# Cutting 33 unread matrix products into 99 narrower ones ahead of the first expert

## The chip, the cores and the metric

The kernel runs on one core of a Trainium2 chip. The metric is the device time of one execution in microseconds (us). Three runs of the kernel before gave 690.85, 692.42 and 748.87 us; their median is 692.42 us. The profiled execution took 690.02 us by the same measure, and 688.4 us of it is the span from the first to the last instruction, so 1.6 us lie around the span.

## The reference, cut to what matters

Two parts follow each other. The first is attention over 8 batches, 8 heads, 576 positions and 64 dimensions, once over positions averaged in fours and once over a narrow band; the second is a mixture of experts on its 4608 rows of 512 numbers:

```python
x = np.ascontiguousarray(attn_out.transpose(0, 2, 1, 3)).reshape(B * S, H * D)
...
logits = x @ w_gate
order = np.argsort(-flat)
for idx in order:                       # greedy, at most cap = N // E = 576 rows for each expert
    ...
    assigned[tok] = e
...
for e in range(E):
    mask = assigned == e
    h = np.maximum(x[mask] @ w1[e], 0.0)
    out[mask] = h @ w2[e]
```

Which row goes to which expert depends on all logits together: an expert that is full passes its rows on. All 8 experts end with 576 rows each.

## The kernel before, in words

The first 244 us of the trace are attention; it leaves the rows x in the chip's main memory and their logits in on-chip memory. Then come eight units, one for each expert that becomes full, in the order in which they do. A unit has four stages. Its **routing** (`Routing.phase`) finds the threshold of the next full expert by counting: comparisons on VectorE (L879), counts as small products on TensorE into the tile pR (L933, L951, L979), and a rank and a list of rows (L990, L991, L1202). Its **gathering** (`Experts.gather`) fetches 576 rows of x by the list in five indirect transfers (`xg`, L1326, issued by GpSimd), turns them with products against the identity (L1343, into pX) and splits them into two 16-bit parts (`xt`, high on ScalarE L1347, low on VectorE L1348). Its **weights** arrive by their own transfers and are split likewise (`wh` L1306, `wl` L1309). Its **products** (`mlp`) are the first layer (L1390, into pH, with the split of its result on ScalarE L1421 and VectorE L1424) and the second (L1438, into pX), whose results are scattered to the output (L1448).

For the first unit nothing can be hidden behind an earlier one: routing is a chain that alternates between VectorE and TensorE, then rows have to be fetched, then turned. In that stretch the kernel gives TensorE products that nobody reads. `Routing.busy` (L905) puts 5 and 8 of them between the last steps of the routing, each 128 x 128 against 288 columns. `Experts.spin` (L1286) puts 33 more of the same size behind the list of rows: 28 ahead of the turning of the first 128 rows, and 5 behind it, ahead of the first real product. They multiply a tile of ones (`one`) with the table `codes` and write one half of a pH buffer, from which nothing is read. This is what "first gathering" and "unread products" mean in this document.

A scheduler sets the order of the instructions on each engine from priorities and dependences. Dependences that only fix the order on one engine are added by hand; those around the change are:

```python
for a, b in ((ex.spins[0], ex.turns[0]), (ex.turns[0], ex.spins[1])):
    for mm in b:
        ro.behind_(mm, a[-1])
...
ro.behind_(ex.products[0], ex.spins[1][-1])
```

So TensorE does the 28, then the four turning products of the first rows (`turns[0]`), then the 5, then the first real product (`products[0]`). pH has two buffers: the first belongs to the 13 unread products of the routing and then to the first real products (f = 0); the second belongs to the 33 unread products and then to the products for f = 1, which therefore wait until the last of the 33 has ended.

Of the kernel before, what the change touches and what calls it, by code (L numbers as in the profile page):

```python
# [1222 lines left out]
class Experts:  # L1223
# [62 lines left out]

    def spin(self, a, b):
        p = self.ps.tile([128, 2, 512], F32, name="pH", bufs=2)
        n = b.shape[1] * b.shape[2]
        mm = [self.nc.tensor.matmul(p[:, 0, :n], a, b.rearrange("p e t -> p (e t)"), start=True, stop=True)  # L1290
              for _ in range(sum(SPIN))]
        self.spins = mm[:SPIN[0]], mm[SPIN[0]:]

    def split(self, raw, first):
# [175 lines left out]
LEAD = -19.0  # L1470
PACE = (0.6, 4, 10.5, 13, 15.3, 17, 18.5, 19.2, 21.5, 24, 26.5, 30, 32.5, 36.5, 37.2, 43.9, 43)
PACES = {2: (8.5, 12.8, 15.8, 17.4, 19.1, 20.7, 22.1, 23, 24.7, 26.5, 28.5, 31, 33, 36.5, 37.2, 43.9, 43)}
SPIN = (28, 5)


def moe_attention(tc, q, k, v, wg, w1, w2, cst, out):
# [173 lines left out]
```

## Time and profile before

| what | us |
|---|---|
| profiled execution | 690.02 |
| its span | 688.4 |
| runs | 690.85, 692.42, 748.87 |
| TensorE busy in the span | 646.2 (94%) |
| VectorE busy | 510.6 (74%) |
| ScalarE busy | 331.9 (48%) |
| attention, up to the first routing | 0 to 244 |
| first routing | 244 to 266 |
| first gathering and turning | 266 to 278 |
| units back to back on TensorE | 278 to 681 |

How to read the rows: times are microseconds from the start of the span, durations of single instructions are nanoseconds. PE is TensorE's product, PEld its load of the 128 x 128 stationary tile, which runs beside products; DVE is VectorE, ACT ScalarE, POOL GpSimd. The ends of products are modelled: a product's duration includes its way through the array, and the next one starts before it ends, so the rate of a row of products is read from their starts. PEclk is the clock granted to TensorE as a share of 2.4 GHz; it takes two levels, 0.50 (1.2 GHz) and 1.00. A timeline row such as "x8" merges eight instructions that follow each other.

### The profile page before, as it was taken

What the parts mean: (1) busy time and instruction counts of PE and PEld (TensorE: products, weight loads), DVE (VectorE), ACT (ScalarE), POOL (GpSimd) and SP (SyncE); (2) the same over time, 40 slices, a digit from 0 to 9 for tenths busy, and PEclk for the clock granted to TensorE, in tenths of its full rate; (3) what the DMA queues carried; (4) which work ended last, traced back from release to release, by engine and by line L of the source; (5) the groups of instructions that cost most, each with busy time, mean ns of one, the idle gap of its engine ahead of it and who ended that gap; (6) DMA issues with size and microseconds to landing.
All of it is one profiled execution on the core that took longest, in us unless ns stands there. A gap on an engine that the chain in (4) does not pass through costs nothing.

```text
span 688.4 us, 21563 instructions
## 1 busy us (share of the span) xinstructions
PE 646.2 (94%) x8781; PEld 454.4 (66%) x8781; DVE 510.6 (74%) x1475; ACT 331.9 (48%) x648; POOL 246.2 (36%) x332
## 2 busy tenths in 40 slices
PE   7999999999899948999999999999999999999993
PEld 5778788788777835765764764764764765755841
DVE  5588889878889887997888896896896966534500
ACT  4578777788676413525325434424424424433410
POOL 4698586676827504005005104113013025011011
PEclk9799999999999957999999999999999999999997
DMA  9988978879857714406339159067067089634001
GB/s 271 223 198 231 242 199 231 233 198 241 239 159 194 230 40 142 173 15 229 141 119 287 47 222 207 24 247 183 25 260 169 25 283 249 233 39 99 2 30 38
DMA packets 138505, 113.87 MB, mean 165 GB/s; under 512 B 89126, under 2 KB 116006, under 8 KB 138408
## 3 DMA queue, kind: packets, MB, share of 16 engines
q1 hardware_dynamic: 130648, 89.71, 47.4%
q0 software_dynamic: 6752, 22.03, 10.3%
q8 instruction: 69, 1.13, 0.7%
q10 hardware_dynamic: 1008, 0.77, 0.4%
q14 instruction: 28, 0.23, 0.1%
HBM read 85.94 MB, written 19.46 MB: 153 GB/s over the span
## 4 chain that ended last, share of the span: by engine, by line
PE 56%; issue 17%; DVE 14%; ACT 6%; POOL 3%; DMA 2%; SPq 0%; POOLq 0%; ACTq 0%; DVEq 0%
PE pX L1438 17%; PE pH L1390 14%; PE g L596 4%; PE s L550 3%; PE g L344 2%; PE pR L933 2%; PE g L575 2%; POOL out_dram L1448 2%; PE g L616 2%; ACT kt L328 2%; DVE wl L1309 1%; POOL xg L1326 1%; DVE qt L326 1%; PE g L420 1%; DVE cmp L879 1%
## 5 line engine op out<-in xcount | busy, mean ns | idle before, releaser
L1390 PE MATMUL pH<-xt,wh 128*128 128x320 f16 (+2 forms) x1040 | 192.0, 284 | 1.1 <-PE pH L1290 0.7
L1438 PE MATMUL pX<-wh,ht 128*128 128x512 f16 (+1 forms) x640 | 178.7, 380 | 0.0
L1438 PEld LDWEIGHTS <-ht 128*128 128x128 f16 (+1 forms) x960 | 83.0, 100 | 93.5 <-issue 2.6
L1390 PE MATMUL pH<-xt,wl 128*128 128x320 f16 (+2 forms) x520 | 144.3, 284 | 0.1
L1438 PE MATMUL pX<-wl,ht 128*128 128x512 f16 (+1 forms) x320 | 117.8, 380 | 0.0
L1390 PEld LDWEIGHTS <-wh 128*128 128x128 f16 x1040 | 98.1, 98 | 29.2 <-issue 4.9
L1448 POOL DMA_INDIRECT out_dram<-y,idx x40 | 40.5, 1012 | 177.0 <-ACT y L1445 119.0
L1421 ACT ACTIVATE ht<-pH 128x512 f16<-128x512 f32 (+1 forms) x128 | 45.5, 407 | 114.7 <-PE pH L1390 114.7
L1309 DVE SCALAR_TENSOR_TENSOR wl<-nat,wh 128x512 f16<-128x512 f32 x128 | 83.5, 685 | 15.5 <-ACT wh L1306 13.3
L1445 ACT ACTIVATE y<-pX 128x512 f32<-128x512 f32 (+1 forms) x40 | 23.8, 594 | 104.1 <-issue 54.1
L1424 DVE SCALAR_TENSOR_TENSOR ht<-pH,ht 128x512 f16<-128x512 f32 (+1 forms) x128 | 52.3, 449 | 26.2 <-ACT ht L1421 25.7
L1306 ACT ACTIVATE wh<-nat 128x1024 f16<-128x1024 f32 (+1 forms) x68 | 67.6, 1002 | 4.3 <-DMA nat<-in_moe_w_dram 4.3
L1326 POOL DMA_INDIRECT xg<-x_dram,idx x40 | 42.5, 1062 | 62.8 <-DVE idx L1219 48.6
L1390 PEld LDWEIGHTS <-wl 128*128 128x128 f16 x520 | 50.2, 98 | 12.6 <-DVE wl L1309 0.4
L585 ACT COPY pt<-g 64x512 f32<-64x512 f32 x71 | 41.2, 580 | 25.2 <-PE g L575 20.4
L596 PE MATMUL g<-vw,pt 128*64 128x65 f32 x1152 | 43.1, 225 | 2.7 <-ACT kt L328 0.8
L596 PEld LDWEIGHTS g<-vw,pt 128*64 128x64 f32 x1152 | 37.6, 137 | 8.6 <-issue 3.0
L1093 POOL MEMSET f<- 128x1 bf16 x8 | 0.8, 106 | 111.9 <-DVE sumf L987 41.1
L344 PE MATMUL g<-ident,nat 128*128 128x128 f32 x256 | 38.9, 281 | 0.2 <-DMA nat<-in_k_dram 0.2
L1355 DVE SCALAR_TENSOR_TENSOR xs<-xg,xs 128x512 f16<-128x512 f32 (+1 forms) x30 | 20.1, 688 | 25.4 <-ACT xs L1354 23.2
L328 ACT COPY kt<-g 64x512 f32<-64x512 f32 (+1 forms) x58 | 35.5, 613 | 6.6 <-PE g L344 5.8
L550 PE MATMUL s<-kt,qt 64*32 64x38 f32 x2304 | 30.2, 206 | 6.2 <-issue 4.8
(242 smaller groups left out, 1132.9 us busy)
## 6 DMA issues: line engine op xcount, KB each, us to landing
nat<-in_moe_w_dram SPq DMA_DIRECT2D x28, 1024.0 KB
vw<-in_v_dram SPq DMA_DIRECT2D x136, 78.0 KB
x_dram<-x SPq DMA_DIRECT2D x36, 256.0 KB
nat<-in_q_dram SPq DMA_DIRECT2D x32, 256.0 KB
nat<-in_k_dram SPq DMA_DIRECT2D x32, 256.0 KB
nat<-in_v_dram SPq DMA_DIRECT2D x28, 256.0 KB
up<-up_dram SPq DMA_DIRECT2D x9, 256.0 KB
nat<-in_moe_w_dram POOLq DMA_DIRECT2D x2, 1024.0 KB
```

Source lines behind the costliest of these rows:

```text
L328: self.nc.scalar.copy(out, in_)
L344: nc.tensor.transpose(p[:, a, :, fp], src[:, 4 * hh + 2 * a + s, 2 * fp:2 * fp + 2].rearrange("p f d -> p (f d)"), self.ident)
L550: nc.tensor.matmul(sv[32 * hp:32 * hp + 32, i, c], qt[r, hp, QW * w:QW * w + QW], kt[r, hp, key0(w):key0(w) + KW], start=False, stop=True, ...
L596: nc.tensor.matmul(o[64 * i:64 * i + 64, 65 * h:65 * h + 65], pt[:, 2 * (h % 2) + i, 2 * g + h // 2].rearrange("p b q -> p (b q)"), self.v ...
L1306: self.wh.append(nc.scalar.activation(hi[:, a:b], r[:, a:b], AF.Copy, scale=sc))
L1309: self.wl = nc.vector.scalar_tensor_tensor(lo[:, a:a + LOP], r[:, a:a + LOP], sc, hi[:, a:a + LOP], op0=OP.mult, op1=OP.subtract)
L1326: self.fetched = nc.gpsimd.indirect_dma_start(out=xg[:n], out_offset=None, in_=self.x, in_offset=bass.IndirectOffsetOnAxis(ap=idx[:n, c:c ...
L1390: mm = nc.tensor.matmul(p[:, s, o:o + s1 - s0], w[d][a][:, 128 * f:128 * f + 128], xt[:, b, d, s0:s1], start=j == 0, stop=j == len(seq) - 1)
L1421: last = nc.scalar.activation(hi, q, AF.Relu)
L1424: low = nc.vector.scalar_tensor_tensor(lo, q, 0.0, hi, op0=OP.max, op1=OP.subtract)
L1438: mm = nc.tensor.matmul(p[o:o + m], ht[:, f, h0:h0 + m], w[4 + f // 2][b][:, 512 * (f % 2):512 * (f % 2) + 512], start=j < parts, stop=j > ...
L1448: i = nc.gpsimd.indirect_dma_start(out=self.out, in_=y[:n], in_offset=None, out_offset=bass.IndirectOffsetOnAxis(ap=idx[:n, c:c + 1], axis=0))
```

## The change

The 288 columns of `codes` are taken in three thirds of 96 columns. Each of the 33 products becomes three, each with its own load of the same stationary tile: 84 ahead of the first turning and 15 behind it. They write the three thirds of the same 288 columns of pH. The number of columns that stream through the array is the same (33 x 288 = 99 x 96 = 9504).

```diff
     def spin(self, a, b):
         p = self.ps.tile([128, 2, 512], F32, name="pH", bufs=2)
-        n = b.shape[1] * b.shape[2]
-        mm = [self.nc.tensor.matmul(p[:, 0, :n], a, b.rearrange("p e t -> p (e t)"), start=True, stop=True)
-              for _ in range(sum(SPIN))]
+        n = b.shape[1] * b.shape[2] // CUTS
+        flat = b.rearrange("p e t -> p (e t)")
+        mm = [self.nc.tensor.matmul(p[:, 0, n * (k % CUTS):n * (k % CUTS) + n], a, flat[:, n * (k % CUTS):n * (k % CUTS) + n],
+                                    start=True, stop=True) for k in range(sum(SPIN))]
         self.spins = mm[:SPIN[0]], mm[SPIN[0]:]
...
-SPIN = (28, 5)
+CUTS = 3
+SPIN = (28 * CUTS, 5 * CUTS)
```

Line numbers of the changed kernel are higher by one behind L1290. On TensorE, around the turning of the first rows, the order before is this (`one` is the tile of ones, `xg` the fetched rows):

```order
L1290 LDWEIGHTS one
L1290 MATMUL pH<-codes,one 128x288
L1343 MATMUL pX<-ident,xg 128x128 x4
L1290 LDWEIGHTS one
L1290 MATMUL pH<-codes,one 128x288
```

and after the change:

```order
L1291 LDWEIGHTS one
L1291 MATMUL pH<-codes,one 128x96
L1344 MATMUL pX<-ident,xg 128x128 x4
L1291 LDWEIGHTS one
L1291 MATMUL pH<-codes,one 128x96
```

The turning stays where it was between the two groups; what stands on either side are 84 and 15 pairs of a load and a product in place of 28 and 5.

The scheduler also moves a few neighbours. On ScalarE, behind the first piece of `xt`, the order before is (`xh` and `xl` are tables of the second routing, copied in two halves each):

```order
L1347 ACTIVATE xt<-pX 128x4x128
L1047 COPY xh<-s 128x288
L1347 ACTIVATE xt<-pX 128x4x128
L1047 COPY xh<-s 128x288
L1047 COPY xl<-s 128x288 x2
L1347 ACTIVATE xt<-pX 128x4x128 x2
```

and after the change:

```order
L1348 ACTIVATE xt<-pX 128x4x128
L1047 COPY xh<-s 128x288 x2
L1047 COPY xl<-s 128x288
L1348 ACTIVATE xt<-pX 128x4x128
L1047 COPY xl<-s 128x288
L1348 ACTIVATE xt<-pX 128x4x128 x2
```

Two of the copies pass from behind the second piece of `xt` to ahead of it. On VectorE, at the end of the first f of the first unit, the order before is (`less` and `flag` are steps of the second routing, `ht` the low part of the layer's result):

```order
L1059 TENSOR_TENSOR oh<-eq,amu 128x288
L943 TENSOR_TENSOR less<-cap,pR 64x8
L1424 SCALAR_TENSOR_TENSOR ht<-pH,ht 128x512
L1424 SCALAR_TENSOR_TENSOR ht<-pH,ht 128x64
L946 TENSOR_TENSOR flag_5647<-pR,less 64x8
```

and after the change:

```order
L1059 TENSOR_TENSOR oh<-eq,amu 128x288
L1425 SCALAR_TENSOR_TENSOR ht<-pH,ht 128x512
L1425 SCALAR_TENSOR_TENSOR ht<-pH,ht 128x64
L943 TENSOR_TENSOR less<-cap,pR 64x8
L946 TENSOR_TENSOR flag_5647<-pR,less 64x8
```

The two `ht` steps pass ahead of `less`. On TensorE the small products of the second routing keep their order and stand behind one to three more products of the first layer, up to the fourth f; from there on, and on GpSimd and SyncE throughout, the orders are the same.

## Rows read from the trace of the kernel before

**Rows 1.** The page: busy time, then 40 slices of the span, tenths.

```profile
PE 646.2 (94%) x8781; PEld 454.4 (66%) x8781; DVE 510.6 (74%) x1475; ACT 331.9 (48%) x648; POOL 246.2 (36%) x332
PE   7999999999899948999999999999999999999993
PEclk9799999999999957999999999999999999999997
```

**Rows 2.** Chain of waits, 266 to 284 us: start, us, what.

```profile
266.54 3.95 DMA xg<-x_dram,idx
...
270.54 0.66 PE pX L1343 x4
271.19 1.74 PE pH L1290 x5
...
272.98 0.38 PE pH L1390 x4
273.36 0.46 PE pX L1343 x4
273.84 0.61 ACT xt L1347
274.47 0.69 DVE xt L1348
...
277.13 0.48 PE pX L1343 x4
277.63 0.39 ACT xt L1347
...
278.06 2.20 PE pH L1390 x15
```

**Rows 3.** The 33 products alone: count, durations in ns, first and last start.

```profile
L1290 PEld LDWEIGHTS <-one x33: 97/98/147, 264.8 to 271.4; 128*128 128x128 bf16 x33
L1290 PE MATMUL pH<-codes,one x33: 286/286/444, 264.8 to 271.5; 128*128 128x288 bf16 x33
```

**Rows 4.** Timeline, 261 to 274 us: start, us, engine, line, idle before and releaser.

```profile
261.98 2.11 PE L905 MATMUL pH<-codes,one 128*128 128x288 bf16 x8
...
264.80 5.08 PE L1290 MATMUL pH<-codes,one 128*128 128x288 bf16 x28
...
270.54 0.66 PE L1343 MATMUL pX<-ident,xg 128*128 128x128 f32 x4 [0.66 <-DMA xg<-x_dram,idx]
...
271.03 0.78 PE L1290 MATMUL pH<-codes,one 128*128 128x288 bf16 x5
...
271.23 0.60 ACT L1347 ACTIVATE xt<-pX 128x512 f16<-128x512 f32 x1 [2.95 <-issue]
...
271.88 0.38 PE L1390 MATMUL pH<-xt,wh 128*128 128x128 f16 x4
...
272.98 0.38 PE L1390 MATMUL pH<-xt,wh 128*128 128x128 f16 x4 [0.72 <-PE pH L1290]
```

**Rows 5.** Stretches: PE, PEld, DVE, ACT, POOL busy, PEclk, DMA share, GB/s.

```profile
260.00:262.00 2.00, 1.53 (x9) 0.65 (x8) 1.64 (x9) 0.00 (x0) 0.00 (x0) 0.50 0.00 0
...
266.00:267.00 1.00, 1.00 (x6) 0.63 (x5) 0.25 (x1) 0.98 (x3) 0.46 (x1) 0.50 0.51 195
267.00:268.00 1.00, 1.00 (x6) 0.61 (x5) 1.00 (x3) 1.00 (x3) 0.69 (x2) 0.57 0.00 0
268.00:269.00 1.00, 1.00 (x11) 0.80 (x9) 1.00 (x3) 0.28 (x1) 0.88 (x1) 1.00 0.72 156
...
273.50:276.00 2.50, 2.50 (x41) 2.48 (x40) 1.53 (x5) 2.07 (x5) 2.24 (x4) 1.00 0.73 205
```

**Rows 6.** The 33 products in a slow and a fast stretch: first and last start.

```profile
L1290 PE MATMUL pH<-codes,one x6: 444/444/444, 265.5 to 266.7; 128*128 128x288 bf16 x6
...
L1290 PE MATMUL pH<-codes,one x10: 286/286/286, 268.5 to 269.6; 128*128 128x288 bf16 x10
```

**Rows 7.** Timeline of TensorE: narrower products, each with its own load.

```profile
21.44 2.66 PE L772 MATMUL g<-wm 128*64 128x64 bf16 x46
...
253.54 0.65 PE L933 MATMUL pR<-ol,level 128*128 128x16 bf16 x18 [1.09 <-DVE ol L1125]
...
273.64 0.61 PE L1390 MATMUL pH<-xt,wl 128*128 128x128 f16 x8
...
274.09 0.61 PE L1390 MATMUL pH<-xt,wh 128*128 128x128 f16 x8
```

**Rows 8.** Stretches of the attention, PE alone: PE busy, PEclk, DMA share, GB/s.

```profile
18.70:22.10 3.40, 2.28 (x79) 0.50 1.16 205
22.10:25.50 3.40, 3.40 (x45) 0.50 0.99 263
25.50:29.00 3.50, 3.50 (x57) 1.00 1.05 189
```

**Rows 9.** Timeline, ScalarE, VectorE and TensorE at the moved steps.

```profile
273.84 0.60 ACT L1347 ACTIVATE xt<-pX 128x512 f16<-128x512 f32 x1 [1.64 <-PE pX L1343]
274.34 0.42 ACT L1047 COPY xh<-s 128x288 int16<-128x288 int16 x1
...
279.15 1.11 PE L1390 MATMUL pH<-xt,wh 128*128 128x320 f16 x7
280.10 0.60 PE L933 MATMUL pR<-oh,level 128*128 128x16 bf16 x18
...
280.74 0.16 DVE L943 TENSOR_TENSOR less<-cap,pR 64x8 f32<-64x8 f32 x1 [0.70 <-PE pR L933]
280.94 0.82 DVE L1424 SCALAR_TENSOR_TENSOR ht<-pH,ht 128x512 f16<-128x512 f32 x2
```

## The prediction

> **What bounds the kernel now.** I read the page first. TensorE is busy for 646.2 of 688.4 us [rows 1], and the slices show it nearly full except for two around 245 to 260 us, the first routing. The clock row beside them falls to 5 and 7 in the same place. So the question is whether the change touches the little that stands between the end of the routing and the first unit.
>
> The second view is the chain of waits there [rows 2]. From 266.54 us it goes through the transfer of the fetched rows, which takes 3.95 us, then at 270.54 through the four turning products, then through TensorE until 272.94, and on through real products, turning and the splits of `xt`, until 278.06. No link is the group of 28 unread products: it lies beside the transfer. The group of 5 is a link, and its share is strange: 1.74 us for five products.
>
> The third view is the timeline of the same stretch [rows 4]. The 28 run from 264.80 to 269.88; then TensorE idles for 0.66 us until the rows land. The four turning products end at 271.19, ScalarE's split runs from 271.23 to 271.83, and the first real products start at 271.88. The 5 stand between, from 271.03. After four real products TensorE idles for another 0.72 us, until 272.98, and this idle time is put down to the last unread product: the products for f = 1 need the pH buffer it writes. That last product starts at 271.5 and lasts 286 ns [rows 3], so it should end at 271.8; its release comes at 272.94 [rows 2], 1.1 us later. No row says why.
>
> The fourth view is the granted clock [rows 5]: 0.50 until 267 us, 0.57 from 267 to 268, 1.00 after. With 0.14 of that microsecond at full speed, the rise came at about 267.86 us, 5.9 us after TensorE began to run without pause on the 8 unread products at 261.98 [rows 4].
>
> **The change, step by step.**
>
> *What a narrower product costs.* Six old products start between 265.5 and 266.7: five steps of 240 ns at 1.2 GHz. Ten start between 268.5 and 269.6: nine steps of 122 ns at 2.4 GHz [rows 6]. No row has 96 columns, so I bound the step from both sides. From below: a third of the old step each, nothing lost. From above: every pair pays a whole load of its tile, 98 ns [rows 3]. In between lie products that also load a tile each [rows 7]: eight of 128 columns take 0.45 us from 273.64 to 274.09, 56 ns each at 2.4 GHz; 18 of 16 columns take at most 0.65 us, 36 ns each, at 1.2 GHz; 46 of 64 columns take at most 2.66 us, 58 ns each, at 1.2 GHz. A line through 56 ns at 128 columns and 122 at 288 gives 43 ns at 96; a line through 58 ns at 64 and 240 at 288 gives 84 ns at most. I take these, since 96 is closest to 64 and 128. Three new ones cost 129 ns against 122, or 252 against 240.
>
> *The front group.* 264.80 to 269.88 with 27 steps before the last start means about 13 slow and 15 fast products. The change adds at most 13 x 12 ns + 15 x 7 ns = 0.26 us, so the group ends by 270.14. The transfer that lands at 270.54 hides it; 0.40 us of the cover remain. Were the cover gone, each further tenth would go straight into the chain.
>
> *The second group.* 15 x 43 = 645 ns against 5 x 122 = 610: +0.03 us. The first real product waits for ScalarE until 271.83 anyway; the old group is through the array's entrance at 271.03 + 0.61 = 271.64, so 0.19 us remain. On the path: 0.
>
> *The late release.* It lies on the chain, so any change goes through. If it came with the last product's end, TensorE would gain the 0.72 us of idle time. If its 1.1 us grew with the count of products from 5 to 15, the delay would be 3.3 us, 2.2 more. The columns, the buffer, the clock and the place are the same as before; I take 0 and keep -0.72 and +2.2 as ends.
>
> *Instructions.* 66 more products and 66 more loads. TensorE's sequencer hands out 18 pairs in 0.65 us [rows 7], 36 ns a pair, so pairs at 43 ns do not starve it. No other engine gets one more instruction, and no transfer changes.
>
> *Moved steps.* On ScalarE two copies of 0.42 us pass ahead of the second `xt`, into a hole of 1.64 us in which ScalarE waited for turning products [rows 9]: nothing. VectorE takes the next step behind that `xt` in both orders, so the copies come no sooner for it. Three real products move ahead of the last turning, where TensorE would wait for VectorE; but the piece behind them waits for ScalarE until 278.02 [rows 2], so nothing is won. On VectorE `ht` (0.82 us) now runs before `less`, in a hole of 0.70 us [rows 9]; the counts that `less` waits for come one product later, (1.11 - 0.30) / 6 = 0.135 us for 320 columns. What is late next is `less` itself, by some 0.6 us, but `flag` stood behind `ht` before and does so now: the second routing moves by at most 0.15 us either way, beside a TensorE that has real products to do. I count 0, with an end of 0.15.
>
> *The sum.* 690.02 + 0 + 0 + 0 = 690.0 us for an execution like the profiled one; ends 689.3 and 692.4 from the release and the moved steps. The two runs beside it took 690.85 and 692.42 us (the third, 748.87, is far off, and the median of 692.42 is the upper of the two). The mean of 690.02, 690.85 and 692.42 is 691.1. **I predict 691.1 us.**
>
> **The rivals.**
>
> *Slower: the clock stays at 1.2 GHz.* The rise might follow from something that three short products give less of than a long one. The point that decides: whether the clock is up before 269 us. Price: 28 times 240 to 252 ns end the front group at 271.5 to 271.9, 1.0 to 1.3 us behind the rows; the second group takes 1.2 us in place of 0.61, +0.6; and if the real products need the same 5.9 us to raise it, running at half speed where TensorE was full (from 273.5 to 276 us [rows 5]), they lose up to half, 2.95 us. Less the idle 0.72 that this fills: 4.0, or 694.0 us. Against it: 46 products of 64 columns stood from 21.44 to 24.1 us at 0.50 [rows 7], and the clock was at 1.00 from 25.5 on [rows 8]; they are narrower still. Chance 0.06.
>
> *Slower: every pair pays for its load.* 84 x 98 ns end the front group at 273.0, +2.5; 15 x 98 = 1.47 against 0.61 less the 0.19 spare, +0.67: 693.2 us. Against it are the 36 and 56 ns of [rows 7], in this kernel with a load each. Chance 0.04. [...]
>
> *Faster: the late release goes.* Should the 1.1 us be tied to the long form of the products, the idle 0.72 us disappears: 689.3 us, or 690.4 with the same offset for the runs. For it: no row shows a resource that is busy then. Against it: the same buffer and wait remain. Chance 0.12.
>
> That the change does not do what it says is excluded by the order of the changed kernel, which holds 99 pairs.
>
> **How the numbers follow.** The forecast has 0.70; the rivals 0.12, 0.06 and 0.04; 0.08 is left for what I do not see. The range runs from 688.8 (the faster rival at 689.3, less a half of the spread seen) to 694.8 (the clock rival at 694.0 on the profiled execution, with most of the offset of the runs). A measurement of this kernel tells about 2% from no change, 13.8 us; every priced case is within 5. Faster by more 0.02, within 0.95, slower by more 0.03; the two small ones are from the unseen 0.08.
>
> **What would show it.** In the changed profile: 99 products in L1291 with first starts near 264.8, steps of 80 to 84 ns before the clock's rise and about 43 behind it; the front group done near 270.0, and an idle of 0.4 to 0.6 us before the turning that still ends with the transfer; PEclk at 1.00 from about 268; the first real product still released by ScalarE; and the products for f = 1 still idle some 0.7 us behind the last unread one. A turning that follows the unread products without idle time, a clock at 0.50 past 270 us, or a step near 98 ns would make the prediction wrong, and each names its rival.

## The result, and the profile after

The changed kernel took 695.27 us (median of 22 runs, 692.34 to 698.32), the kernel before 691.11 us beside it (median of 22). The medians lie 4.2 us apart. The ratio of the runs, without the one of 748.87 us, is 1.0055, with a 95% interval of 1.0038 to 1.0072: 0.55% slower. The forecast was 691.1 us, the range 688.8 to 694.8.

The profiled execution took 698.32 us, its span is 696.7 us. Its page, in the lines that answer to [rows 1]:

```profile
PE 650.5 (93%) x8847; PEld 459.5 (66%) x8847; DVE 512.1 (74%) x1475; ACT 332.5 (48%) x648; POOL 249.0 (36%) x332
PE   7899899999899856999999999999999999999994
PEclk9999999999999956899999999999999999999997
```

66 products and 66 loads more, as the change says. The timeline of TensorE in the first gathering answers to [rows 4]:

```profile
269.08 4.01 PE L1291 MATMUL pH<-codes,one 128*128 128x96 bf16 x84
274.26 0.66 PE L1344 MATMUL pX<-ident,xg 128*128 128x128 f32 x4 [1.17 <-DMA xg<-x_dram,idx]
274.76 0.71 PE L1291 MATMUL pH<-codes,one 128*128 128x96 bf16 x8
276.61 0.32 PE L1291 MATMUL pH<-codes,one 128*128 128x96 bf16 x2 [1.14 <-issue]
278.08 0.56 PE L1291 MATMUL pH<-codes,one 128*128 128x96 bf16 x5 [1.15 <-issue]
278.93 1.01 PE L1391 MATMUL pH<-xt,wh 128*128 128x128 f16 x8 [0.29 <-ACT xt L1348]
...
285.88 0.70 PE L1391 MATMUL pH<-xt,wh 128*128 128x320 f16 x4 [0.36 <-ACT xt L1348]
```

The 84 run without a gap and end at 273.09; TensorE idles 1.17 us until the rows land (forecast 0.4 to 0.6). So far nothing is on the path that was not there before. Then the 15 products behind the turning come in three batches with gaps of 1.14 and 1.15 us that the profile puts down to "issue": TensorE waited for nothing that it shows. ScalarE, in the same stretch:

```profile
270.37 2.25 ACT L1307 ACTIVATE wh<-nat 128x512 f16<-128x512 f32 x4
278.28 0.60 ACT L1348 ACTIVATE xt<-pX 128x512 f16<-128x512 f32 x1 [5.66 <-remote]
```

Its first `xt` needs the four turning products, which end at 274.26 + 0.66 = 274.92. It starts at 278.28, 3.36 us later; in [rows 4] it started 0.04 us behind them. The word "remote" does not mean another core, there is only one: the profile found no end of work near 278.28 that could be the releaser. The trace has a record of TensorE's semaphore at 278.25, 3.3 us behind the end of the turning; so the report itself came late. The chain of waits, which answers to [rows 2], has the same hole under another name:

```profile
272.62 5.63 another core or an unknown queue
278.28 0.61 ACT xt L1348
278.93 1.01 PE pH L1391 x8
```

The stretches with the clock, as in [rows 5], show what followed:

```profile
269.00:270.00 1.00, 1.00 (x28) 1.00 (x25) 0.64 (x4) 0.26 (x1) 0.00 (x0) 0.84 0.79 279
...
276.00:277.00 1.00, 0.32 (x2) 0.10 (x1) 0.19 (x1) 0.00 (x0) 1.00 (x2) 0.57 0.75 213
277.00:278.00 1.00, 0.00 (x0) 0.10 (x1) 0.00 (x0) 0.00 (x0) 1.00 (x2) 0.50 0.68 229
...
281.00:282.00 1.00, 1.00 (x13) 1.00 (x11) 0.54 (x1) 0.75 (x2) 0.00 (x0) 0.50 1.01 373
...
283.00:284.00 1.00, 1.00 (x19) 0.99 (x18) 0.57 (x5) 0.60 (x1) 0.00 (x0) 1.00 0.99 389
```

The clock rose in time, at about 269.3. It fell at about 276.1, after TensorE had stood idle from 273.09 to 274.26 and again from 275.47, and came back near 283.0. Four us of real products and turnings ran at 1.2 GHz: eight of 128 columns take 1.06 us at 281.44 and 0.61 at 283.07.

**Where the time lies.** From the first routing product (244.37 before, 248.66 after) to the first block of 320 columns (278.06 and 285.88) it is 33.69 and 37.22 us, +3.53. From the rows' landing to the first real product: 1.34 and 4.67, +3.33. From there to the block: 6.18 and 6.95, +0.77, the slow clock less the idle time that is gone. Ahead of the landing: 26.17 and 25.60, -0.57. The spans differ by 8.3 us, though: 4.29 of it lies ahead of the first routing product, in the attention, where nothing was changed. In the executions below the first routing product starts between 242.98 and 251.15 us, so that is scatter from one execution to the next.

### The profile page after: what moved, and what is told of

The parts are those of the page before. It is cut to its first block, busy times and chain, and to the rows that moved or that the text cites. A ratio compares the mean times of both kernels' runs of the same rounds, so it can differ in the third digit from the quotient of the medians.

```text
span 696.7 us, 21696 instructions
## 1 busy us (share of the span) xinstructions
PE 650.5 (93%) x8847; PEld 459.5 (66%) x8847; DVE 512.1 (74%) x1475; ACT 332.5 (48%) x648; POOL 249.0 (36%) x332
## 3 DMA queue, kind: packets, MB, share of 16 engines
q8 instruction: 70, 1.15, 0.7%
## 4 chain that ended last, share of the span: by engine, by line
PE 36%; issue 15%; DVE 6%; POOL 3%; ACT 2%; another core or an unknown queue 1%; POOLq 0%; DVEq 0%; ACTq 0%
PE pX L1439 17%; PE pH L1391 14%; PE pR L933 2%; POOL out_dram L1449 2%; DVE wl L1310 1%; POOL xg L1327 1%; ACT wh L1307 1%; DVE cmp L879 1%; ACT ht L1422 1%; PE pR L1202 1%; DVE ht L1425 1%; PE g L640 0%; PE pX L1344 0%; DVE less L943 0%
```

## The experiments

All but the copies use one edit, which takes count and width of each group from a table (where the second group is empty, the first real product stands behind the turning instead); below only the table is given:

```diff
+        self.spins = tuple(
+            [self.nc.tensor.matmul(p[:, 0, n * (k % (288 // n)):n * (k % (288 // n)) + n], a,
+                                   flat[:, n * (k % (288 // n)):n * (k % (288 // n)) + n], start=True, stop=True)
+             for k in range(count)] for count, n in SPIN)
...
-SPIN = (28 * CUTS, 5 * CUTS)
+SPIN = ((84, 96), (5, 288))
```

Ratios are to the kernel before on the same chip. "Report" is the moment at which an engine's semaphore tells others that its work is done; "late" means behind the end of the work in the profile. Where late reports of a whole execution are counted, it is the trace's records of semaphores that come over 0.3 us late or are missing. Most of these are missing, and the count shifts by some ten with the way in which records are matched with instructions.

### Which group costs it: chip 3

**e1_front**, `SPIN = ((84, 96), (5, 288))`.

> 84 products of 96 columns ahead of the turning, 5 of 288 columns behind it: the front group alone is cut, and the neighbours stand in the order of the changed kernel. Theory A (what counts is how many unread products, each with its load, stand ahead of the turning, whatever follows): the report of the first turning is some 3 us late as in the changed kernel, time +3 to +4 us over the kernel before. Theory B (what counts is the 15 narrow pairs behind the turning): report on time, 0 to +0.3 us. Theory C (the moved neighbours): +3 to +4 us, but without a late report.

**e2_back**, `SPIN = ((28, 288), (15, 96))`.

> 28 products of 288 columns ahead of the turning, 15 of 96 columns behind it: the second group alone is cut, and the neighbours stand in the order of the kernel before. Theory A: 0 +- 0.5 us against the kernel before. Theory B: TensorE stands still for some 3 us among the 15, time +3 to +4 us. Theory C: 0.

**e3_noback**, `SPIN = ((84, 96), (0, 96))`.

> 84 products of 96 columns ahead of the turning and none behind it. Theory A: the report of the turning is late all the same, +3 us. Theory B: the stall goes, and with it the late release that the kernel before has too: -0.7 to 0 us against the kernel before, and PEclk stays at 1.00 from its rise on. Theory C: +3 us.

**e4_few**, `SPIN = ((28, 96), (5, 96))`.

> 28 products of 96 columns ahead of the turning and 5 of 96 behind it: as many instructions as before with a third of the columns. Theory A: report of the turning on time. Theory B: a stall no longer than before (1.1 us). Both: the front group ends near 268 us and the clock may not be up by then or may fall again in the wait for the rows, so that the first real products run at 1.2 GHz: 0 to +3 us.

Measured, in this order: 1.0024 (0.9998 to 1.0050), 1.0023 (0.9992 to 1.0053), 1.0040 (1.0016 to 1.0065) and 0.9988 (0.9960 to 1.0016). Only e3_noback is told from the kernel before, and by time e1_front and e2_back are alike: the +3 to +4 us that theory A expected of e1_front did not show in its median, which is 1.1 us higher. What tells them apart is the traces. TensorE in e1_front:

```profile
269.50 0.66 PE L1344 MATMUL pX<-ident,xg 128*128 128x128 f32 x4 [1.35 <-DMA xg<-x_dram,idx]
269.99 0.78 PE L1291 MATMUL pH<-codes,one 128*128 128x288 bf16 x5
274.20 1.01 PE L1391 MATMUL pH<-xt,wh 128*128 128x128 f16 x8 [3.44 <-ACT xt L1348]
```

The old five behind, and still `xt` comes 3.4 us late. In e3_noback there is nothing behind, and the gaps are inside the group ahead and inside the turning:

```profile
265.69 4.20 PE L1291 MATMUL pH<-codes,one 128*128 128x96 bf16 x74
...
271.77 0.33 PE L1291 MATMUL pH<-codes,one 128*128 128x96 bf16 x4 [0.43 <-issue]
273.25 0.30 PE L1344 MATMUL pX<-ident,xg 128*128 128x128 f32 x1 [1.15 <-issue]
274.69 0.80 PE L1344 MATMUL pX<-ident,xg 128*128 128x128 f32 x3 [1.14 <-issue]
```

In e2_back and e4_few the turning is reported on time. From the first routing product to the first block of 320 columns the four profiles take 36.62, 35.75, 38.24 and 33.56 us, against 33.69 in the kernel before. The +2.1 of e2_back goes with something else: its rows landed 2.21 us behind the front group, and the clock was at 0.50 from 274 to 280 us (eight products of 128 columns take 1.06 us at 278.74 and 0.61 at 280.29). So the late report belongs to the group ahead, and there to the count of products rather than the columns: 84 narrow ones bring it, 28 wide ones and 28 narrow ones do not. Theory B fell, and so did theory C, which had no late report.

### Is it the gathers beside them: chip 9

My next theory was F: while GpSimd issues the gathers, TensorE's instructions and reports come slowly, and what counts is how many fall there.

**e5_short**, `SPIN = ((84, 32), (5, 288))`.

> 84 products of 32 columns ahead and 5 of 288 behind: as many TensorE instructions ahead of the turnings as in the changed kernel, but done sooner. Theory F (reports of finished TensorE work and the supply of its instructions are slow while GpSimd issues the gathers, so what counts is how many TensorE instructions fall into that stretch): the front group ends about 2.5 us after its start, most of it before GpSimd's first gather, the turnings are reported at most 1 us late, and the time is 0 to +1.5 us against the kernel before, the positive part only if the granted clock falls in the wait for the rows. Theory S (the lateness comes from the count that one semaphore is raised by in one step, 84 or 88): the first turnings are reported 3.3 us late all the same and the time is +1 to +4 us.

**e6_drop5**, `SPIN = ((28, 288), (0, 288))`.

> 28 products of 288 columns ahead and none behind the turnings. Theory F: the five wide products behind the first turnings are themselves a small part of the load, the first routing product follows ScalarE's first xt instead of the late release, and the time is 0 to -1 us against the kernel before; the 0.72 us of idle time between the last unread product and the first routing product is gone or becomes a wait for xt. Rival (the release of the first routing product is late whatever stands in front of it): its 0.7 us of idle time stays, and the time is within 0.5 us of before or above it.

**e7_hold**, the changed kernel with one dependence more: the second gather waits for the last unread product, and the other three follow it on GpSimd.

```diff
+                for z in ex.fetches[1:2]:
+                    tc.add_manual_dep(z.ins, ex.spins[1][-1].ins.name, ...
```

> The changed kernel, 84 and 15 products of 96 columns, with GpSimd's gathers of the rows of the second to the fifth unit held until the last unread product has ended. Theory F: with no gather issued beside them the first turnings are reported on time (within 0.2 us of their end), and the 15 unread products run without the stalls of 1.1 us between batches; the rows of the later units land some 4 us later, so the time itself is +1 to +4 us against the kernel before and says little. Theory S, and any other cause within TensorE's own instructions: the turnings are reported 3.3 us late and the stalls are there all the same.

**e8_wide**, `SPIN = ((16, 512), (0, 512))`, with another moving operand.

> 16 unread products of 512 columns ahead (with another moving operand, an earlier level of the first weights, nothing reads the results) and none behind: about the columns of the front group before in 32 TensorE instructions instead of 56. Theory F: no late report is left in the stretch, and the time is 0 to -1.5 us against the kernel before. Theory S: 0 to -0.7 us, since only the five products behind are gone.

Measured, in this order: 1.0007 (0.9982 to 1.0032), 1.0017 (0.9990 to 1.0044), 1.0058 (1.0029 to 1.0088; its rows come 4 us later, as said) and 0.9996 (0.9972 to 1.0021). In none is a report late. That looks like proof of F. But in all the later units, where these kernels do what the others do, the reports were on time as well: 0 to 4 late ones of VectorE, ScalarE and TensorE in a whole execution, against some 50 to 70 in each of the six earlier profiles. So these four could not tell F from a better chip. Nor did e6_drop5 and e8_wide gain the 0 to 1.5 us that F expected.

### The same four kernels on one chip: chip 12

**e9_after** is the changed kernel, **e10_before** the kernel before, **e11_hold** is e7_hold and **e12_short** e5_short.

> The changed kernel once more, with the next three on one chip, since the four kernels without late reports so far had run on another chip than the five with them. Theory F (what counts is how many TensorE instructions fall into the stretch of GpSimd's gathers): the first turnings are reported about 3.3 us late, the unread products stall for 1.1 us twice, and the time is +3 to +4.5 us against the kernel before. Theory K (the late reports belong to the chip and not to the program): on a chip that has none the 15 products run in 0.8 us without a stall and the time is within 1 us of the kernel before; on a chip that has them this kernel shows them, and so do the next three.

> The kernel before, on the same chip as the changed one. Theory F: the first routing product starts 0.7 us after the last unread product's end, since its release is 1.1 us late. Theory K on a chip without late reports: no such gap here and none in the changed kernel.

> 84 and 15 products of 96 columns with GpSimd's gathers two to five held until the last unread product, on the same chip as the changed kernel. Theory F: no report is over 0.2 us late and the 15 products run in 0.8 us, while the changed kernel beside it stalls. Theory K: it shows what the changed kernel shows on this chip.

> 84 products of 32 columns ahead and 5 of 288 behind, on the same chip as the changed kernel. Theory F: the turnings are reported on time or at most 1 us late, and the time is 0 to +1 us against the kernel before. Theory K: it shows the late reports that the changed kernel shows on this chip, +1 to +4 us on a chip that has them.

Measured: the changed kernel 692.32 us against 691.96, ratio 1.0012 (0.9985 to 1.0039); e12_short 1.0019 (0.9994 to 1.0043); e10_before and e11_hold have one run each, 693.25 and 697.18 us (its rows come late again). The timeline of the changed kernel:

```profile
273.36 0.66 PE L1344 MATMUL pX<-ident,xg 128*128 128x128 f32 x4 [0.77 <-DMA xg<-x_dram,idx]
273.85 0.80 PE L1291 MATMUL pH<-codes,one 128*128 128x96 bf16 x15
274.70 0.61 PE L1391 MATMUL pH<-xt,wh 128*128 128x128 f16 x8
...
280.41 0.70 PE L1391 MATMUL pH<-xt,wh 128*128 128x320 f16 x4 [0.36 <-ACT xt L1348]
```

This is what the prediction described: no gap, the first real product 1.34 us behind the turning's start. In the kernel before on this chip the late release of [rows 4] is gone too: the real products follow the last unread one without the 0.72 us, here with the clock at 0.50 from 274 to 276 us.

```profile
274.18 1.40 PE L1290 MATMUL pH<-codes,one 128*128 128x288 bf16 x5
275.38 1.06 PE L1390 MATMUL pH<-xt,wh 128*128 128x128 f16 x8
276.23 1.06 PE L1343 MATMUL pX<-ident,xg 128*128 128x128 f32 x4
```

F alone fell; theory K (the chip) held, with at most four late reports in each of the four.

### F on a chip with late reports: chip 5

> The changed kernel a third time, to see which kind of chip this call has. On a chip with late reports (more than ten reports of VectorE, ScalarE and TensorE over 0.3 us late behind GpSimd's gathers): turnings 3.3 us late, two stalls of 1.1 us in the 15 products, +2.5 to +4.5 us against the kernel before. On a chip without: no stall, and within 1.5 us of it.

> 84 and 15 products of 96 columns, GpSimd's gathers two to five held until the last unread product. Theory F+K (late reports need both such a chip and GpSimd's gathers beside the products): no late report at the first turnings even where the changed kernel shows 3.3 us. Theory K alone (the chip, whatever GpSimd does): as late as in the changed kernel. On a chip without late reports it says nothing.

> 84 products of 32 columns ahead and 5 of 288 behind. Theory F+K: the front products end before most of the gathers, so the first turnings are reported at most 1.2 us late even where the changed kernel shows 3.3 us. Theory K alone: about 3.3 us late, as 84 instruction pairs stand ahead of them. On a chip without late reports it says nothing.

**e13_after**, the changed kernel: 697.39 us against 692.37, ratio 1.0066 (1.0040 to 1.0091), some 60 late reports; the +5.0 us by the medians is a little over the +4.5 that I had allowed.

```profile
271.57 4.20 PE L1291 MATMUL pH<-codes,one 128*128 128x96 bf16 x81
276.13 0.25 PE L1291 MATMUL pH<-codes,one 128*128 128x96 bf16 x2 [0.36 <-issue]
...
277.58 0.49 PE L1344 MATMUL pX<-ident,xg 128*128 128x128 f32 x3 [0.39 <-issue]
...
280.48 1.05 PE L1291 MATMUL pH<-codes,one 128*128 128x96 bf16 x11 [1.19 <-issue]
281.37 1.01 PE L1391 MATMUL pH<-xt,wh 128*128 128x128 f16 x8
```

**e14_hold**, the same 99 products on the same chip, with some 60 late reports in the later units, but the second gather issued only at 276.81. TensorE:

```profile
270.08 4.43 PE L1291 MATMUL pH<-codes,one 128*128 128x96 bf16 x84
275.24 0.66 PE L1345 MATMUL pX<-ident,xg 128*128 128x128 f32 x4 [0.73 <-DMA xg<-x_dram,idx]
275.73 0.80 PE L1291 MATMUL pH<-codes,one 128*128 128x96 bf16 x15
276.58 0.61 PE L1392 MATMUL pH<-xt,wh 128*128 128x128 f16 x8
```

No gap, nothing late. **e15_short**: 84 pairs ahead, but mostly done before the gathers:

```profile
273.65 1.12 PE L1344 MATMUL pX<-ident,xg 128*128 128x128 f32 x4 [2.83 <-DMA xg<-x_dram,idx]
274.56 1.41 PE L1291 MATMUL pH<-codes,one 128*128 128x288 bf16 x5
275.76 0.63 PE L1391 MATMUL pH<-xt,wh 128*128 128x128 f16 x4
277.44 0.58 PE L1391 MATMUL pH<-xt,wh 128*128 128x128 f16 x4 [1.05 <-PE pH L1291]
```

The turning is on time, and what is late is the last unread product, as in [rows 4]. F and K hold together, in one profile each: it takes such a chip and gathers beside the products. Theory S, the height of the semaphore's step, fell: as many products, the 84 and the four of the turning, stand ahead of the report here as in e1_front. (e14_hold and e15_short have one run each, 698.93 and 696.83 us.)

### Gathers or transfers, and how many: chip 8

**e16_wide** is e8_wide again. **e17_plain** is the changed kernel with

```diff
+                if first and c:
+                    z = nc.sync.dma_start(out=xg[:n], in_=self.x[128 * c:128 * c + n])
```

and a wait of these for the first gather. **e18_mid** has `SPIN = ((56, 144), (5, 288))`.

> 16 unread products of 512 columns ahead of the turnings and none behind, once more, to have it on a chip with late reports if this call gets one (more than ten reports over 0.3 us late behind the gathers of the later units tell that). There, theory F+K: the turnings are reported less than 0.5 us late, the first routing product follows ScalarE's first xt by 0.7 us, and the time is 0 to -2 us against the kernel before, which loses 0.7 us to its late release. On a chip without late reports: -1 to +1 us, as before.

> The changed kernel's 84 and 15 products, but the rows of the second to the fifth unit are fetched by plain transfers of consecutive rows on SyncE's queue, after the first unit's rows have landed; they are rows of other tokens, as many bytes. GpSimd issues one indirect gather and then its four plain weight transfers. Theory G (GpSimd's indirect gathers are what slows TensorE's instructions and reports on such a chip): first turnings reported at most 0.5 us late, no stall of 1.1 us. Theory T (the transfers of rows and weights do, whoever issues them): as late as in the changed kernel, 2.6 to 3.3 us. On a chip without late reports it says nothing.

> 56 products of 144 columns ahead and 5 of 288 behind: the columns of the kernel before, with 61 pairs of instructions between its 33 and the 89 of the kernel with 84 narrow ones ahead. On a chip with late reports, theory F+K: later than with 28 ahead (1.1 us at the last unread product) and less late than with 84 (3.4 us at the first turnings), +0.5 to +2 us against the kernel before. On a chip without: within 1 us of it.

This chip has late reports too (some 50 to 70). e16_wide: 0.9985 (0.9958 to 1.0012), first turnings on time. e18_mid: 1.0046 (1.0017 to 1.0076), +2.7 us by the medians where I had expected +0.5 to +2, and as late as with 84:

```profile
270.64 0.66 PE L1344 MATMUL pX<-ident,xg 128*128 128x128 f32 x4 [1.37 <-DMA xg<-x_dram,idx]
271.13 0.78 PE L1291 MATMUL pH<-codes,one 128*128 128x288 bf16 x5
275.16 1.01 PE L1391 MATMUL pH<-xt,wh 128*128 128x128 f16 x8 [3.25 <-ACT xt L1348]
```

e17_plain (one run, 696.76 us, as four groups of rows land late): TensorE first,

```profile
271.77 0.66 PE L1349 MATMUL pX<-ident,xg 128*128 128x128 f32 x4 [0.51 <-DMA xg<-x_dram,idx]
272.26 0.80 PE L1291 MATMUL pH<-codes,one 128*128 128x96 bf16 x15
273.11 0.61 PE L1396 MATMUL pH<-xt,wh 128*128 128x128 f16 x8
```

then GpSimd beside it, and for comparison the first and last gather of GpSimd in the changed kernel's first profile:

```profile
268.41 0.99 POOL L1332 DMA_INDIRECT xg<-x_dram,idx  x1 [4.43 <-ACT idx L1217]
269.80 1.51 POOL L1252 DMA_DIRECT2D nat<-in_moe_w_dram  x2 [0.39 <-issue]
271.60 1.50 POOL L1255 DMA_DIRECT2D nat<-in_moe_w_dram  x2 [0.30 <-issue]
```

```profile
270.82 1.00 POOL L1327 DMA_INDIRECT xg<-x_dram,idx  x1 [4.43 <-ACT idx L1217]
...
275.97 1.01 POOL L1327 DMA_INDIRECT xg<-x_dram,idx  x1 [0.30 <-issue]
```

61 pairs run between the one gather and the turning, 30 of them and the 15 behind it beside GpSimd's four plain issues, and nothing is late. That speaks for theory G as against T. One reserve: the plain transfers of the rows ran only from about 272 us on, so that the rows' transfers beside the first group were not tried; the weights' were, with the DMA engines 0.70 and 1.00 busy from 270 to 272.

### All runs by one count

Pairs of load and product of the unread groups that start between GpSimd's first gather and the first turning, counted in the trace, and the time from the first turning's start to the start of ScalarE's `xt` (0.7 us when nothing is late, 1.1 where the turning itself ran at 1.2 GHz):

| late-report chips | pairs | turning to `xt`, us |
|---|---|---|
| e4_few | 0 | 0.69 |
| e16_wide | 11 | 0.70 |
| e2_back | 13 | 1.15 |
| e15_short | 17 | 1.15 |
| kernel before | 20 | 0.69 |
| e18_mid | 29 | 3.87 |
| e1_front | 43 | 4.06 |
| changed kernel | 45 | 4.02 |
| e13_after, the same | 52 | 3.84 |
| e3_noback | 60 | 2.28, and 2.45 of gaps ahead |
| e14_hold, gathers held | 59 | 0.69 |
| e17_plain, gathers replaced | 61 | 0.69 |
| other chips: e9_after | 58 | 0.69 |

In these executions, one for each row, it is a step between 20 and 29 pairs, not a slope; the count was chosen after the runs. e18_mid, which I had put in between, is 3.2 us late. And the report then comes when the gathers are over: the last one's issue ends at 276.98 in the changed kernel and `xt` starts at 278.28; in e1_front it is 272.30 and 273.56, in e13_after 279.48 and 280.72, in e18_mid 273.46 and 274.51. So 1.1 to 1.3 us behind the last gather, however many products stood ahead.

One rival can be read off the traces: that TensorE waits for its code to be loaded. The packets of the two queues that the page marks "instruction" come at 270.66 and 271.22 us in the changed kernel, and the next at 286.95; none falls into the gaps from 275.47 to 278.08.

The cost stays in this stretch. From the first block of 320 columns to the end the kernels without held gathers take 410.0 to 410.2 us on chips 9 and 12 and 410.2 to 410.8 on the others, so the late reports of the later units cost under 1 us together.

## Why the prediction was wrong

- **The step that failed: the late release**, with **Instructions** beside it. The prediction had the 1.1 us between the last unread product's end and its release in its rows, wrote "No row says why", and took it as unchanged: 0, with +2.2 as an end. The runs show a step there, though not its cause: with 20 pairs ahead of the turning only the five products behind it were reported late, and on chip 12 not even those. With 45 pairs on a chip with late reports what is late is the turning's report, by 3.3 us, for which ScalarE's split, and so every real product, waits. "Pairs at 43 ns do not starve it" came from 18 pairs in 0.65 us [rows 7], a stretch of the routing without a gather. Beside the gathers the rest of the 84 still ran at 43 ns, but the 15 came as 8, 2 and 5 with 1.1 us between.
- **The range** ended at 694.8. The end of +2.2 let the delay grow on one release, in place. In fact the whole 3.33 us lay on the path, and the clock fell in the standstill: 0.77 more behind it. +3.53 in the profiles, +4.2 in the medians. The low end of the range does not follow from its own words: 689.3 less half of the 2.4 us between the runs is 688.1 and not 688.8. And the offset of the runs taken in full, 1.1 us, would have put the high end at 695.1, still short of 695.27.
- **The clock rival** had the wrong moment. The clock rose in time beside the narrow products (269.3); it fell in the standstill behind them (276.1).
- **What held**: the price of a narrow product. 15 of them in e9_after take 0.80 us, of which the last is 0.206: (0.80 - 0.206) / 14 = 42 ns, forecast 43; at 1.2 GHz the front group's steps are 80 ns in e9_after, forecast at most 84. The front group ended ahead of the rows by 1.17 us (0.77 in e9_after; forecast 0.4). The larger margin is luck: the clock rose 0.2 us after the start of the group and not 3.1 as in the kernel before. "Every pair pays for its load" did not come. On chip 12, where no report of this stretch is late, the forecast of no change was right: 1.0012, 692.32 us against the 691.1.
- **Not shown**: the moved steps (0 +- 0.15) are below what any of these runs resolves.

So the answer hangs on the chip: two comparisons on chips with late reports gave +0.55% and +0.66%, one on a chip without gave +0.12% with zero in its interval. Each chip was measured at one time only, so that "chip" may also be something that belongs to that machine at that hour. What it is about it, no run shows.

What makes the reports late on such a chip is open. One thing in the trace tells a report from its record: in the kernel before, the trace has no record of the turning's report before 272.94, though ScalarE had started on that report at 271.23 [rows 4]; there the record was late or lost and not the report. The traces also lose records on just these chips: of about 2580 reports of VectorE, ScalarE and TensorE 45 to 62 have no record there, on chips 9 and 12 at most one. Of the 16 landing records of each of the five gathers the changed kernel's first profile holds 3, 5, 4, 9 and 16, e16_wide, in which no turning is late, 2, 4, 4, 11 and 16, and e9_after all 16 each time. So records go missing beside the gathers there, with many pairs or few. No run shows whether the recording holds TensorE up or whether both have another cause: every timed execution has its clock and span recorded, so none tells what an unrecorded one would do.

No version was shown to beat both kernels. e4_few (0.9988) and e16_wide (0.9985) come nearest to beating the kernel before, both with few instructions beside the gathers and on chips with late reports, but both intervals hold 1.

## What to carry to other kernels

A release that comes 1 us behind its producer's end, with no row to say why, may stand close to a step like the one between 20 and 29 pairs here: ask what in that stretch the change doubles, and let the range hold the case that the late report moves ahead to a step on the path, where it cost 3.3 us here. Count the instructions of filler as well as its time: beside gathers, 16 products of 512 columns kept the turning on time (`xt` 0.70 us behind its start, e16_wide) on a chip where 56 of 144 did not (3.87 us, e18_mid). Before a mechanism is believed, run the kernel in question and its cure on the same chip: four runs here agreed with a theory only because their chip did not show the effect at all.

## What the runs showed of the hardware

- In four of the six sets of runs (the first, and those on chips 3, 5 and 8), some 50 to 75 reports of VectorE, ScalarE and TensorE in an execution are recorded over 0.3 us late or not at all, at most two of them ahead of GpSimd's first gather; on chips 9 and 12 the same programs have 0 to 4. In part only the record is late or missing. In the first gathering the wait is real, up to 3.4 us (e1_front).
- On such a chip 20 pairs of load and product ran beside the gathers with the turning reported on time (`xt` 0.69 us behind its start, kernel before), and with 29 the report was 3.2 us late (3.87 us, e18_mid; one profile each). In the changed kernel, e3_noback and e13_after TensorE then gets 1 to 8 pairs at a time, up to 1.2 us apart, and runs on freely 1.0 to 1.1 us behind the end of the last gather's issue.
- A pair of load and product with 96 columns takes 42 to 43 ns at PEclk 1.00 and 80 ns at 0.50 (e9_after), a third of the 122 and 240 ns of 288 columns within 2 ns [rows 6]. "2.4 GHz" and "1.2 GHz" name these two levels of PEclk, at which 288 columns take 122 and 240 ns.
